# Attention scores of all units as plain float32 products on the two halves of the rows

## The chip, the cores and the metric

The kernel runs on one core of a Trainium2 chip. The metric is the device time of one execution in microseconds (us). A core has a matrix engine (TensorE, PE in the profile; its loads of stationary operands are PEld), VectorE (DVE), ScalarE (ACT), GpSimd (POOL), and SyncE (SP), which here issues nearly all DMAs. A program's instructions stand in a fixed order on each engine, and an instruction that waits holds up all behind it on that engine.

## The reference, cut to what matters

```python
# attention: B=2, H=8, S=576, D=64
scores = scale * np.matmul(q, k.transpose(0, 1, 3, 2))
rel = np.log1p(np.abs(pos[:, None] - pos[None, :]))
x = (rel / np.log1p(np.maximum(pos[:, None], 1.0)))[..., None]
bias = np.maximum(x @ w1 + b1, 0.0) @ w2          # one bias per head, 576 x 576
scores = scores + bias.transpose(2, 0, 1)[None]
attn = softmax(scores)                            # over the last axis
out = attn @ v                                    # then x of 1152 tokens x 512
# two feed-forward layers
x = (silu(x @ w_gate) * (x @ w_val)) @ w_out      # d_ff 1536
x = softplus(x @ w_in) @ w_out2                   # d_ff 2048
```

## The kernel before, in words

The program has three stages on the matrix engine: the bias of all heads, the attention, and the two feed-forward layers, which come last and which the diff does not touch.

**Bias.** 36 steps, one after the other. In each, DVE and ACT make four hidden tiles (`hidden`), PE multiplies them by `W2` on four column strips (`second`, L289), ACT scales the result into a staging tile (`keep`, L302), and SP issues a DMA that spreads the staging tile over rows of `bias[c]`, from SBUF to SBUF. Eight staging tiles go round: four halves of `early[0]` and `early[1]`, and four tiles of the pool `stp`. The last eight steps fill `bias[3]` (`bias_91` in the order lists).

**Attention.** A unit is two heads of one batch (`pr`, `b`); there are eight, in the order of `UNITS`. A unit has two subs (rows 0 to 255 and 256 to 575) and nine chunks of 128 rows by 576 keys; the chunk `mix` holds 64 rows of both heads. `run_slot` is called once for each chunk and does, in this order: the chunk's scores on PE (`scores`), copies of transposes of the slot before (`gather`), bias and minimum on DVE (`biased`, L377), the exponential of the chunk before on ACT and its normalization on POOL (`softmax`, L391 and L399), one or two groups of transposes of a sub that ended three slots ago (`transposes`, L426, four blocks of 128 x 128 as a rule), and, where all of a sub's groups have been copied, its products with the values (`values`, L453). The order on PE, ACT, DVE, POOL and SP is the order in which the code is written (`tc.manual_schedule`). Scores have two PSUM buffers (`psS`): the scores of a slot wait until `biased` of two slots before has read its buffer. Four slots of unit 0 (`EARLY`) are run between bias steps, the others after them.

**Scores of units 1 to 7.** Both halves of the 128 rows hold a copy of the head's 64 dimensions. `prepare_k` and `prepare_q` split keys and queries into float32r high and low parts (`kst`, `qh`, `ql`) on ACT, DVE and POOL (L204, L206, L210), two steps in each slot. A chunk is then four float32r products over all 128 rows (`ql` and `qh` for each half of the 576 keys), the mixed chunk eight (L356).

**Scores of unit 0.** `plain_scores` (L328) takes plain float32 products: each head stands once, in its own half of the rows, and two chunks of different heads are issued together, so that their products use different halves.

**Loads.** `load_k(0)`, `load_v(units[0])` and the first table come at the start. The keys of unit 1 and 256 columns of its queries are loaded between bias steps (`NEXT`), its other query columns and its values at slot 4. A load of both copies of one tensor is two DMAs of 64 rows (L162), 288 KB each; unit 0's are one DMA of 128 rows each (L180).

**Pools.** After the bias steps the pool `ep1` is opened at the right end of SBUF, where `stp` and other tiles of the bias stage stood; the second of the two `mixes` (`m_919`) lies in it, and POOL clears a strip of each (L615).

Of the kernel before, what the change touches and what calls it, by code (L numbers as in the profile page):

```python
# [11 lines left out]
F32 = mybir.dt.float32  # L12
# [7 lines left out]
P = 128  # L20
# [20 lines left out]
NEXT = (20, 28)  # L41

# [3 lines left out]
KHIGH, KLOW = "va", "ppvp"  # L46
QHIGH, QLOW = "vvvavva", "ppppp"
# [53 lines left out]
def tile_kernel(ctx: ExitStack, tc, qT, kT, vS, wb, wg, wv, wo, wi, wo2, table, out):  # L101
# [27 lines left out]
    with ExitStack() as actx:  # L129
# [4 lines left out]
        rawp = opener(right)("qkraw", 1, side="right")  # L134
        kp = pool("kp", 2)
        qp = pool("qp", 1)
# [20 lines left out]
        qraw = pool("qraw", 1)  # L157
        psS = pool("psS", 2, space=PSUM)

        def load(r, src, pr, b, cols=slice(None)):  # L160
            for d in range(2):
                sp.dma_start(  # L162
                    out=r[D * d : D * (d + 1), :, cols],
                    in_=src[b, 2 * pr : 2 * pr + 2, :, cols].rearrange("h d s -> d h s"),
                )

        def load_k(i):

            pr, b = UNITS[i]
            u = dict(i=i, pr=pr, b=b)  # L170
            if i == 1:
                kr = early[3]
            elif i > 2:
                kr = bias[0][:, :2]
            else:
                kr = rawp.tile([P, 2, S], F32, tag="kr", name="kr")
            if i == 0:

                for t, src in ((0, kT), (1, qT)):
                    sp.dma_start(out=kr[:, t], in_=src[b, 2 * pr : 2 * pr + 2].rearrange("h d s -> (h d) s"))  # L180
                u["qr"] = kr[:, 1]
                kr = kr[:, 0]
            else:
                load(kr, kT, pr, b)
            u["kr"] = kr
            return u

        def load_q(u, cols=slice(None)):
            if "qr" not in u:
                u["qr"] = qraw.tile([P, 2, S], F32, tag="qr", name="qr")  # L190
            load(u["qr"], qT, u["pr"], u["b"], cols)
# [10 lines left out]
        def high(h, src, by="a"):  # L202
            if by == "a":
                nc.scalar.copy(h, src)  # L204
            else:
                nc.vector.tensor_copy(h, src)  # L206

        def low(l, h, src, by="p"):
            eng = nc.gpsimd if by == "p" else nc.vector
            eng.tensor_tensor(l, src, h.bitcast(F32), op=ALU.subtract)  # L210

        def prepare_k(u):


            kst = u["kst"] = kp.tile([P, 2, S], F32R, tag="kst", name="kst")
            kr = u["kr"]
            for a in range(2):
                high(kst[:, a], kr[:, a], KHIGH[a])
                yield
                for hf in range(2):  # L220
                    rows, cols = slice(D - D * hf, P - D * hf), slice(HALF * hf, HALF * (hf + 1))
                    low(kst[rows, a, cols], kst[rows, a, cols], kr[rows, a, cols], KLOW[2 * a + hf])
                yield

        def job(sub):
            chunks = [(0, 0), (1, 0), ("mix",), (0, 1), (1, 1)] if sub else [(0, 0), (1, 0), (0, 1), (1, 1)]
            return dict(sub=sub, chunks=chunks, sm=smp.tile([P, 4, 5], F32, name="sm"), es=[], last=[], at={})

        def prepare_q(u, sub):


            qr = u["qr"]
            if u["i"] == 0:
                u[sub] = dict(u, **job(sub))
                return
            width = 704 if sub else 512
            qh = qp.tile([P, width], F32R, tag=f"qh{sub}", name="qh")
            ql = qp.tile([P, width], F32R, tag=f"ql{sub}", name="ql")
            if sub == 0:
                parts = [(0, 0, 0, 256), (1, 256, 0, 256)]  # L240
            else:
                parts = [(0, 0, 256, 320), (1, 384, 256, 320)]
                nc.gpsimd.memset(qh[:, 320:384].bitcast(F32), 0.0)
                nc.gpsimd.memset(ql[:, 320:384].bitcast(F32), 0.0)
            u[sub] = dict(u, qh=qh, ql=ql, **job(sub))
            for j, (a, o, s0, w) in enumerate(parts):
                high(qh[:, o : o + w], qr[:, a, s0 : s0 + w], QHIGH[2 * sub + j])
                yield
                low(ql[:, o : o + w], qh[:, o : o + w], qr[:, a, s0 : s0 + w], QLOW[2 * sub + j])
                yield  # L250
# [5 lines left out]
        stp = pool("stp", 4)  # L256
        early = [xp.tile([P, 2, S], F32, tag=f"a{i}", name=f"early{i}") for i in range(4, 8)]
        spare_st = [t[:, i] for t in early[:2] for i in range(2)]
# [39 lines left out]
        def keep(s, pb):  # L298
            c, t = divmod(s, 8)
            i = order.index(s) % 8  # L300
            st = stp.tile([P, S], F32, name="st") if i % 2 else spare_st[i // 2]
# [9 lines left out]
        def plain_scores(u, *ns):  # L311


            sub, made = u["sub"], []
            for n in ns:
                ch = u["chunks"][n]
                if ch[0] == "mix":
                    heads, bt = [(0, 512, D), (1, 256, D)], bias[4][:, u["pr"]]
                else:
                    a, c = ch  # L320
                    heads, bt = [(a, 256 * sub + D * (sub and a) + P * c, P)], bias[2 * sub + c][:, 2 * u["pr"] + a]
                made.append((psS.tile([P, 2, 512], F32, tag="S", name="ps"), bt, heads))
            for step in range(2):
                for ps, _, heads in made:
                    for a, o, m in heads:
                        rows = slice(D * a, D * (a + 1))
                        hf = (step + a) % 2
                        nc.tensor.matmul(  # L328
                            ps[rows if m == D else slice(None), hf, :HALF],
                            u["qr"][rows, o : o + m],  # L330
                            u["kr"][rows, HALF * hf : HALF * (hf + 1)],
                            start=True,
                            stop=True,
                        )
            return [(ps, bt) for ps, bt, _ in made]

        def scores(u, n):

            sub, pr = u["sub"], u["pr"]
            ch = u["chunks"][n]  # L340
            ps = psS.tile([P, 2, 512], F32, tag="S", name="ps")
            if ch[0] == "mix":
                heads = [(0, 256), (1, 320)]
                bt = bias[4][:, pr]
            else:
                a, c = ch
                heads = [(a, (448 if sub else 256) * a + P * c)]
                bt = bias[2 * sub + c][:, 2 * pr + a]

            if u["i"] == 0:  # L350
                return plain_scores(u, n)[0]
            kst = u["kst"]
            parts = [(t, a, o) for t in ("ql", "qh") for a, o in heads]
            for hf in range(2):
                for i, (t, a, o) in enumerate(parts):
                    nc.tensor.matmul(  # L356
                        ps[:, hf, :HALF],
                        u[t][:, o : o + P],
                        kst[:, a, HALF * hf : HALF * (hf + 1)],
                        start=i == 0,  # L360
                        stop=i == len(parts) - 1,
                    )
            return ps, bt
# [151 lines left out]
        prep = prepare_q(units[0], 0)  # L515
        before = None
        ahead = []
        slot = 0

        def run_slot():  # L520
            nonlocal turned, done, prep, before, slot
            if slot < len(chunks):
                i, sub, n = chunks[slot]
                if n == 0:
                    for _ in prep:
                        pass
                    if sub == 0:
                        if 0 < i < 2 * NP - 1:
                            units.append(load_k(i + 1))
                        if i == NP:  # L530
                            flat = lambda ap: ap.rearrange("p a s -> p (a s)")
                            pairs[2:] = [flat(bias[c][:, 2 * a : 2 * a + 2]) for a in range(2) for c in (2, 3)]
                            mixes[1] = flat(bias[4][:, :2])[:, : 5 * P]
                            nc.gpsimd.memset(mixes[1][:, S:], 0.0)
                        prep = prepare_q(units[i], 1)
                    elif i + 1 < 2 * NP:
                        load_q(units[i + 1], slice(256 if i == 0 else 0, S))
                        load_v(units[i + 1])
                        prep = itertools.chain(prepare_k(units[i + 1]), prepare_q(units[i + 1], 0))
# [21 lines left out]
            for _ in range(2):  # L561
                next(prep, None)
# [578 lines left out]
```

## Time and profile before

| | |
|---|---|
| time of three runs | 601.05, 601.07, 601.9 us; median 601.07 |
| the profiled execution | 601.18 us, of which the span of the trace is 599.4 us |
| busy share of the span | PE 97%, PEld 86%, DVE 76%, ACT 62%, POOL 17% |
| bias stage, attention, feed-forward layers | to about 59 us, to about 200 us, to the end |

Matmuls are pipelined and overlap, so that a busy PE says little; what counts is from the start of one block of products to the start of the next.

### The profile page before, as it was taken

The page shows a single profiled execution, that of the slowest core. Times are in us where ns is not written, and L with a number is a line of the kernel's source. Part 1 is how long each engine was busy: PE and PEld are TensorE (multiplying, and loading weights), DVE is VectorE, ACT ScalarE, POOL GpSimd, SP SyncE. Part 2 cuts the span into 40 slices and gives each one's busy share as a digit, 9 for nine tenths or more (in the row PEclk, how much of TensorE's full clock was granted, in tenths as well). Part 3 has the DMA queues.
Part 4 walks back from the last instruction along what each step waited for, and adds up shares of the span by engine and source line. Part 5 has one row for each costly group of instructions (what it writes and reads, how often), then busy time and mean ns, then how long its engine had stood idle before and what let it go on. Part 6 is the DMA issues. An engine that isn't in the chain of part 4 may idle for free.

```text
span 599.4 us, 11363 instructions
## 1 busy us (share of the span) xinstructions
PE 580.0 (97%) x4274; PEld 515.1 (86%) x4274; DVE 454.9 (76%) x977; ACT 374.6 (62%) x713; POOL 104.6 (17%) x156
## 2 busy tenths in 40 slices
PE   8998399999999999999999999999999999999997
PEld 5444188888887999999999999999989989988986
DVE  6998278878888899888679834679998976983432
ACT  6999187888888877665467525248835734732520
POOL 0001387878995000000000000000000000000000
PEclk9999699999999999999999999999999999999999
DMA  5999734444334243323325222222434340410012
GB/s 191 205 204 204 154 80 111 109 109 109 81 85 152 72 141 98 112 73 108 105 71 176 91 86 70 72 71 72 140 109 136 107 136 7 139 36 1 1 51 107
DMA packets 47414, 62.71 MB, mean 105 GB/s; under 512 B 4480, under 2 KB 35712, under 8 KB 47360
## 3 DMA queue, kind: packets, MB, share of 16 engines
q1 hardware_dynamic: 47216, 61.98, 37.0%
q8 instruction: 33, 0.54, 0.4%
q14 instruction: 21, 0.17, 0.1%
q10 hardware_dynamic: 144, 0.02, 0.0%
HBM read 49.01 MB, written 2.36 MB: 86 GB/s over the span
## 4 chain that ended last, share of the span: by engine, by line
PE 86%; DVE 4%; DMA 3%; POOL 3%; ACT 2%; issue 1%; POOLq 0%; ACTq 0%; SPq 0%
PE pw L748 37%; PE pw L1056 16%; PE pw L699 12%; PE pb L289 6%; PE po L453 5%; PE ps L356 5%; DMA bias<-st 3%; PE pt L426 3%; POOL e L399 1%; PE warm L590 1%; POOL ql L210 1%; DVE bias L377 1%; DVE e L377 1%; ACT at L433 1%; DVE at L433 0%
## 5 line engine op out<-in xcount | busy, mean ns | idle before, releaser
L1056 PE MATMUL pw<-oh,g2h 128*128 128x512 f32 x144 | 56.2, 390 | 0.0
L1056 PE MATMUL pw<-oh,g2l 128*128 128x512 f32 x144 | 56.2, 390 | 0.0
L1056 PE MATMUL pw<-ol,g2h 128*128 128x512 f32 x144 | 56.1, 390 | 0.0
L377 DVE CUSTOM_DVE_ANT_0 e<-ps,bias 128x576 f32<-128x576 f32 x44 | 33.0, 750 | 20.6 <-PE ps L328 12.9
L289 PE MATMUL pb<-r,wb_sb 128*32 128x288 f32 x576 | 47.4, 412 | 0.8 <-ACT st L302 0.7
L699 PE MATMUL pw<-gl,sh 128*128 128x384 f32 x144 | 48.2, 335 | 0.0
L699 PE MATMUL pw<-gh,sl 128*128 128x384 f32 x144 | 48.2, 334 | 0.0
L699 PE MATMUL pw<-gh,sh 128*128 128x384 f32 x144 | 48.2, 334 | 0.0
L281 DVE TENSOR_SCALAR r<-G 128x576 f32<-128x576 f32 x108 | 47.3, 526 | 0.0
L673 DVE SCALAR_TENSOR_TENSOR x<-raw,x 128x512 int32<-128x512 int32 x68 | 46.3, 688 | 0.9
L433 ACT COPY at<-pt 128x512 f32<-128x512 f32 (+2 forms) x69 | 36.3, 548 | 15.4 <-PE pt L426 15.0
L399 POOL TENSOR_SCALAR e<-e,sm 128x576 f32<-128x576 f32 x44 | 33.9, 780 | 64.3 <-DVE sm L396 58.1
L356 PE MATMUL ps<-kst,ql 128*128 128x288 f32 x140 | 43.2, 337 | 1.1 <-DVE sm L377 0.4
L289 PEld LDWEIGHTS pb<-r,wb_sb 128*32 128x32 f32 x576 | 22.5, 109 | 25.0 <-DVE r L281 9.1
L426 PE MATMUL pt<-ident,e 128*128 128x128 f32 x188 | 31.7, 277 | 10.4 <-POOL e L399 10.4
L453 PE MATMUL po<-at,v 128*64 128x256 f32 (+3 forms) x384 | 36.9, 332 | 1.1 <-DVE at L433 0.8
L356 PE MATMUL ps<-kst,qh 128*128 128x288 f32 x140 | 37.4, 295 | 0.0
L1094 DVE TENSOR_TENSOR acc<-pw,acc 128x512 f32<-128x512 f32 x27 | 17.5, 685 | 25.1 <-PE pw L1056 25.1
L391 ACT ACTIVATE e<-e,sm 128x576 f32<-128x576 f32 x44 | 34.4, 781 | 3.4 <-DVE sm L377 2.5
L670 DVE TENSOR_SCALAR x<-x 128x512 int32<-128x512 int32 x68 | 28.8, 428 | 10.1 <-ACT x L669 5.9
L426 PEld LDWEIGHTS pt<-ident,e 128*128 128x128 f32 x188 | 24.0, 143 | 12.5 <-POOL e L399 10.9
L356 PEld LDWEIGHTS ps<-kst,ql 128*128 128x128 f32 x140 | 25.4, 188 | 9.9 <-DVE sm L377 5.0
(276 smaller groups left out, 1674.5 us busy)
## 6 DMA issues: line engine op xcount, KB each, us to landing
raw<-in_wo_dram SPq DMA_DIRECT2D x28, 512.0 KB, 3.6
raw<-in_wi_dram SPq DMA_DIRECT2D x16, 512.0 KB, 3.8
raw<-in_wv_dram SPq DMA_DIRECT2D x12, 512.0 KB, 4.2
raw<-in_wg_dram SPq DMA_DIRECT2D x12, 512.0 KB, 3.6
bias<-early SPq DMA_DIRECT2D x16, 288.0 KB, 7.7
bias<-st SPq DMA_DIRECT2D x16, 288.0 KB, 8.4
qr<-in_qT_dram SPq DMA_DIRECT2D x12, 288.0 KB, 4.1
v<-in_vS_dram SPq DMA_DIRECT2D x8, 384.0 KB, 3.4
```

The lines of the kernel that those rows point to most:

```text
L281: nc.vector.tensor_scalar(r, G[:, w0 : w0 + S], PB[:, n : n + 1], 0.0, op0=ALU.add, op1=ALU.max)
L289: nc.tensor.matmul(pb[32 * ct : 32 * ct + 32, hf, :HALF], W2, rs[ct][:, HALF * hf : HALF * (hf + 1)], start=True, stop=True,)
L356: nc.tensor.matmul(ps[:, hf, :HALF], u[t][:, o : o + P], kst[:, a, HALF * hf : HALF * (hf + 1)], start=i == 0, stop=i == len(parts) - 1,)
L377: nc.vector.tensor_tensor_reduce(out=e[:, :S].rearrange("p (a n) -> p a n", a=2), in0=ps[:, :, :HALF], in1=bt.rearrange("p (a n) -> p a n" ...
L399: nc.gpsimd.tensor_scalar(e, e, sm[:, 3, i : i + 1], 1.0, op0=ALU.mult, op1=ALU.mult)
L426: nc.tensor.transpose(pt[:, P * w : P * (w + 1)], e, ident)
L433: marks[eng, u["i"], u["sub"]] = copy(at[:, :w], pt[:, :w]).ins
L453: nc.tensor.matmul(u["po"][D * a : D * (a + 1), o : o + n], v[:, D * t : D * (t + 1)], at[:, i : i + n], start=piece == 0 and o == 0, stop ...
L673: nc.vector.scalar_tensor_tensor(yi, lw, 29, yi, op0=ALU.logical_shift_right, op1=ALU.bitwise_or)
L699: nc.tensor.matmul(ps[:, :n], w[:, k], x, start=first and k == 0 and i == 0, stop=last and k == NK - 1 and i == 2)
L748: nc.tensor.matmul(ps[:, hf, :HALF], a[:, o + k], b[:, HALF * hf : HALF * (hf + 1)], start=start and k == 0 and i == 0, stop=k == 1 and i ...
L1056: nc.tensor.matmul(ps, g, w.rearrange("p k f -> p (k f)"), start=f == 0 and i == 0, stop=f == 3 and i == 2)
```

## The change

All units' scores become plain float32 products. Keys and queries of every unit, unit 0's too, are loaded twice, a copy in each half of the rows. A chunk is now two products, one in each half of the rows, for the two halves of the keys; the mixed chunk is four, each on a quarter of the array. All high and low parts go, with the instructions that make them. Unit 1's keys and queries are loaded at the start, ahead of the first bias DMA; a later unit's keys, queries and values at the first chunk of the second sub of the unit before it. The staging tiles are eight halves of the four `early` tiles, and both `mixes` lie in `tmpp`.

```diff
+        kqp = pool("kqp", 2)
...
+        def load_kq(i):
+            pr, b = UNITS[i]
+            u = dict(i=i, pr=pr, b=b)
+            for name, src in (("kr", kT), ("qr", qT)):
+                u[name] = kqp.tile([P, 2, S], F32, tag=name, name=name)
+                load(u[name], src, pr, b)
             return u
...
-        stp = pool("stp", 4)
+        staging = itertools.cycle([t[:, i] for t in early for i in range(2)])
...
-            kst = u["kst"]
-            parts = [(t, a, o) for t in ("ql", "qh") for a, o in heads]
-            for hf in range(2):
-                for i, (t, a, o) in enumerate(parts):
-                    nc.tensor.matmul(
-                        ps[:, hf, :HALF],
-                        u[t][:, o : o + P],
-                        kst[:, a, HALF * hf : HALF * (hf + 1)],
-                        start=i == 0,
-                        stop=i == len(parts) - 1,
-                    )
+                parts, bt = [(0, 0, 512), (1, 1, 256), (0, 1, 512), (1, 0, 256)], bias[4][:, pr]
...
+                parts = [(a, hf, o) for hf in range(2)]
+            for a, hf, o in parts:
+                rows = slice(D * hf, D * (hf + 1))
+                to, m = (slice(D * a, D * (a + 1)), D) if ch[0] == "mix" else (slice(None), P)
+                nc.tensor.matmul(
+                    ps[to, hf, :HALF],
+                    u["qr"][rows, a, o : o + m],
+                    u["kr"][rows, a, HALF * hf : HALF * (hf + 1)],
+                    start=True,
+                    stop=True,
+                )
...
-        units, late = [load_k(0)], []
+        units, late = [load_kq(0)], []
         load_v(units[0])
+        units.append(load_kq(1))
...
+                    if i and sub and i + 1 < 2 * NP:
+                        units.append(load_kq(i + 1))
                         load_v(units[i + 1])
...
-            for i, mp in enumerate((tmpp, ep1)):
-                mixes.append(mp.tile([P, 5 * P], F32, name=f"m{i}"))
+            for i in range(2):
+                mixes.append(tmpp.tile([P, 5 * P], F32, name=f"m{i}"))
```

On PE, in unit 1, after the products with the values of unit 0's first sub (`e` and `m` are exponentials, `pt` their transposes, `ps` scores), before:

```order
L453 MATMUL po<-at,vt_99 64x256 x2
L356 MATMUL ps<-kst,ql 128x288
L356 MATMUL ps<-kst,qh 128x288
L356 MATMUL ps<-kst,ql 128x288
L356 MATMUL ps<-kst,qh 128x288
L426 MATMUL pt<-ident,e_909 128x128
L426 MATMUL pt<-ident,e_910 128x128
L426 MATMUL pt<-ident,m_917 128x128
L426 MATMUL pt<-ident,e_909 128x128
```

and of the change, the same place and the next slot:

```order
L350 MATMUL po<-at,vt_93 64x256 x2
L253 MATMUL ps<-kr,qr 128x288 x2
L323 MATMUL pt<-ident,e_881 128x128
L323 MATMUL pt<-ident,e_882 128x128
L323 MATMUL pt<-ident,m_889 128x128
L323 MATMUL pt<-ident,e_881 128x128
L253 MATMUL ps<-kr,qr 128x288 x2
```

The blocks stand in the same order; where four products over the whole array stood there are two over half of its rows, still between transposes over the whole array.

On POOL, at the end of the bias stage, where unit 0's chunks are normalized (TENSOR_SCALAR) and the mixed tiles cleared (MEMSET), with what each waits for (DMAHW is a landing of a DMA), before:

```order
L399 TENSOR_SCALAR e_112<-e_112,sm 128x576 [waits Activation_49]
L615 MEMSET m_917 128x64 [waits DMAHW1_49,Activation_49]
L615 MEMSET m_919 128x64 [waits DMAHW6_49,DMAHW7_49,DMAHW3_49,DMAHW1_49]
L399 TENSOR_SCALAR e_112<-e_112,sm 128x576 [waits DVE_49,Activation_49]
L210 TENSOR_TENSOR kst<-early_131,kst 64x288 [waits DMAHW2_49,DVE_49,Pool_49]
```

and of the change:

```order
L296 TENSOR_SCALAR e_106<-e_106,sm 128x576 [waits Activation_49]
L493 MEMSET m_889 128x64 [waits DMAHW1_49,Activation_49]
L493 MEMSET m_891 128x64 [waits PE_49]
L296 TENSOR_SCALAR e_106<-e_106,sm 128x576 [waits DVE_49,Activation_49]
L296 TENSOR_SCALAR e_881<-e_881,sm 128x576 [waits DVE_49,Activation_49]
```

The second clearing no longer waits for DMAs, and the subtractions for unit 1's keys behind it are gone.

On SP, from the start to the first bias DMA, before:

```order
L264 DMA G<-in_table_dram 128x1064
L180 DMA kr<-in_kT_dram 128x576
L180 DMA kr<-in_qT_dram 128x576
L197 DMA v<-in_vS_dram 128x4x192
L199 DMA vt_99<-in_vS_dram 64x2x64
L200 DMA vt_99<-in_vS_dram 64x64
L309 DMA bias_92<-early_128 16x4x576 x2
```

and of the change:

```order
L191 DMA G<-in_table_dram 128x1064
L155 DMA kr<-in_kT_dram 64x2x576 x2
L155 DMA qr<-in_qT_dram 64x2x576 x2
L171 DMA v<-in_vS_dram 128x4x192
L173 DMA vt_93<-in_vS_dram 64x2x64
L174 DMA vt_93<-in_vS_dram 64x64
L155 DMA kr<-in_kT_dram 64x2x576 x2
L155 DMA qr<-in_qT_dram 64x2x576 x2
L235 DMA bias_86<-early_116 16x4x576 x4
```

Eight loads of 64 rows stand where two of 128 rows stood, and four loads of unit 1 that stood among the bias DMAs (L162) are gone from there.

## Rows read from the trace of the kernel before

**Rows 1.** The page's chain that ended last, shares of the span by engine.

```profile
PE 86%; DVE 4%; DMA 3%; POOL 3%; ACT 2%; issue 1%; POOLq 0%; ACTq 0%; SPq 0%
```

**Rows 2.** Busy time in stretches: PE, PEld, DVE, ACT, POOL, then granted clock, DMA share, GB/s.

```profile
2.00:9.00 7.00, 7.00 (x52) 5.79 (x53) 3.87 (x9) 3.00 (x5) 0.00 (x0) 1.00 0.79 280
8.00:18.00 10.00, 9.96 (x120) 4.75 (x114) 10.00 (x24) 8.88 (x14) 0.00 (x0) 1.00 0.50 138
20.00:57.00 37.00, 36.27 (x444) 17.38 (x434) 36.82 (x89) 35.80 (x58) 0.85 (x1) 1.00 1.05 205
72.00:76.00 4.00, 3.87 (x21) 2.60 (x20) 1.98 (x5) 2.21 (x5) 3.96 (x6) 0.67 0.15 44
92.00:108.00 16.00, 15.58 (x136) 13.04 (x135) 13.36 (x42) 12.63 (x32) 12.56 (x18) 1.00 0.39 101
```

**Rows 3.** The chain that ended last, 57 to 76 us: start, length, what.

```profile
57.29 9.80 DMA bias<-st
67.09 3.11 issue
...
70.35 0.73 POOL e L399
...
75.81 0.80 PE ps L356 x4
```

**Rows 4.** Timeline, 60 to 75 us: who stood idle, and until what, in brackets.

```profile
70.20 0.15 POOL L615 MEMSET m<- 128x64 f32 x1 [11.59 <-issue]
...
71.14 0.48 PE L426 MATMUL pt<-ident,e 128*128 128x128 f32 x1 [10.35 <-POOL e L399]
...
73.87 0.76 DVE L377 CUSTOM_DVE_ANT_0 e<-ps,bias 128x576 f32<-128x576 f32 x1 [11.50 <-PE ps L328]
```

**Rows 5.** DMA queues, 74 to 79 us: packets, MB, share of 16 engines' time.

```profile
q1 hardware_dynamic: 288, 0.59, 44.4%
```

**Rows 6.** The chain that ended last, 77 to 143 us.

```profile
77.36 2.31 PE po L453 x20
...
107.03 0.71 POOL ql L210
...
110.90 2.31 PE po L453 x20
113.21 0.73 PE ps L356 x4
113.94 0.44 PE pt L426 x4
114.37 0.53 PE ps L356 x4
...
116.75 1.05 PE ps L356 x8
...
126.59 2.31 PE po L453 x20
...
143.15 2.31 PE po L453 x20
```

**Rows 7.** Timeline of PE alone in narrow windows at unit 0's plain products.

```profile
38.41 0.41 PE L289 MATMUL pb<-r,wb_sb 128*32 128x288 f32 x2
38.75 0.51 PE L328 MATMUL ps<-kr 64*128 64x288 f32 x2
...
39.10 0.41 PE L328 MATMUL ps<-kr 64*128 64x288 f32 x2
...
59.66 0.41 PE L328 MATMUL ps<-kr 64*64 64x288 f32 x2
...
59.90 0.41 PE L328 MATMUL ps<-kr 64*64 64x288 f32 x2
60.24 0.33 PE L426 MATMUL pt<-ident,e 128*128 128x128 f32 x1
...
60.41 0.38 PE L426 MATMUL pt<-ident,e 128*128 128x128 f32 x2
```

More of the change, by code (lines that the diff above doesn't have):

```diff
@@ L156, in tile_kernel, with load @@
         new_pairs("ep0", 2)
-        qraw = pool("qraw", 1)
         psS = pool("psS", 2, space=PSUM)
-        def load(r, src, pr, b, cols=slice(None)):
+        def load(r, src, pr, b):
             for d in range(2):
                 sp.dma_start(
-                    out=r[D * d : D * (d + 1), :, cols],
-                    in_=src[b, 2 * pr : 2 * pr + 2, :, cols].rearrange("h d s -> d h s"),
+                    out=r[D * d : D * (d + 1)], in_=src[b, 2 * pr : 2 * pr + 2].rearrange("h d s -> d h s")
                 )
-        def load_k(i):
+        def load_kq(i):
             pr, b = UNITS[i]
             u = dict(i=i, pr=pr, b=b)
[L171 to L185, printed above, removed]
-            return u
[L188 to L191, printed above, removed]
+            for name, src in (("kr", kT), ("qr", qT)):
+                u[name] = kqp.tile([P, 2, S], F32, tag=name, name=name)
+                load(u[name], src, pr, b)
+            return u
         def load_v(u):
@@ L225, in job @@
-        def job(sub):
-            chunks = [(0, 0), (1, 0), ("mix",), (0, 1), (1, 1)] if sub else [(0, 0), (1, 0), (0, 1), (1, 1)]
[L227 to L250, printed above, removed]
@@ L252, in tile_kernel, with job @@
+        def job(u, sub):
+            chunks = [(0, 0), (1, 0), ("mix",), (0, 1), (1, 1)] if sub else [(0, 0), (1, 0), (0, 1), (1, 1)]
+            u[sub] = dict(u, sub=sub, chunks=chunks, sm=smp.tile([P, 4, 5], F32, name="sm"), es=[], last=[], at={})
         sctx = actx.enter_context(ExitStack())
@@ L299, in keep @@
             c, t = divmod(s, 8)
-            i = order.index(s) % 8
-            st = stp.tile([P, S], F32, name="st") if i % 2 else spare_st[i // 2]
+            st = next(staging)
             nc.scalar.activation(
@@ L309, in keep @@
                     sp.dma_start(out=bias[c][D * a + t : D * a + t + 61 : 4], in_=st[a::2])
[L311 to L327, printed above, removed]
-                        nc.tensor.matmul(
[L329 to L333, printed above, removed]
-                        )
-            return [(ps, bt) for ps, bt, _ in made]
         def scores(u, n):
@@ L342, in scores @@
             if ch[0] == "mix":
-                heads = [(0, 256), (1, 320)]
-                bt = bias[4][:, pr]
+                parts, bt = [(0, 0, 512), (1, 1, 256), (0, 1, 512), (1, 0, 256)], bias[4][:, pr]
             else:
                 a, c = ch
[L347 to L351, printed above, removed]
-            kst = u["kst"]
-            parts = [(t, a, o) for t in ("ql", "qh") for a, o in heads]
-            for hf in range(2):
-                for i, (t, a, o) in enumerate(parts):
-                    nc.tensor.matmul(
-                        ps[:, hf, :HALF],
-                        u[t][:, o : o + P],
-                        kst[:, a, HALF * hf : HALF * (hf + 1)],
-                        start=i == 0,
-                        stop=i == len(parts) - 1,
-                    )
+                o, bt = 256 * sub + D * (sub and a) + P * c, bias[2 * sub + c][:, 2 * pr + a]
+                parts = [(a, hf, o) for hf in range(2)]
[9 more added lines that the diff above has]
+                )
             return ps, bt
@@ L524, in run_slot @@
                 if n == 0:
[L525 to L537, printed above, removed]
+                    if slot == 4:
+                        load_v(units[1])
+                    if i and sub and i + 1 < 2 * NP:
+                        units.append(load_kq(i + 1))
                         load_v(units[i + 1])
-                        prep = itertools.chain(prepare_k(units[i + 1]), prepare_q(units[i + 1], 0))
+                    if i == NP and sub == 0:
+                        flat = lambda ap: ap.rearrange("p a s -> p (a s)")
+                        pairs[2:] = [flat(bias[c][:, 2 * a : 2 * a + 2]) for a in range(2) for c in (2, 3)]
+                    job(units[i], sub)
                 u = units[i][sub]
-                if ahead:
-                    got = ahead.pop()
-                elif i == 0 and u["chunks"][n][0] == 0:
-                    got, then = plain_scores(u, n, n + 1)
-                    ahead.append(then)
-                else:
-                    got = scores(u, n)
+                got = scores(u, n)
             for w in done:
```

36 lines of the change are left out of this document (2 added, 34 removed).

## The prediction

> **What bounds the kernel now.** I read the chain that ended last first: PE has 86% of it [rows 1], so the question in every stretch is when PE may start its next block. The chain then shows one place where PE does not decide, the change from the bias stage to the attention [rows 3]. From 57 to 67 us it lies on a bias DMA, and the engines start again at 70.2 us. The timeline says who stood there [rows 4]: POOL idle for 11.59 us ahead of clearing the second mixed tile, PE for 10.35 us ahead of a transpose that needs POOL's normalization, DVE for 11.50 us. POOL's wait is marked "issue"; the order list says what it is, landings of DMAs that read the staging tiles. So the last bias row lands at about 70.2 us. The stretches say why so late: from 20 to 57 us the DMA engines are full (share 1.05, 205 GB/s), while from 8 to 18 us they are half idle [rows 2]. After the landing the chain needs another 5.6 us, nearly all POOL (normalizations, low parts of unit 1's keys and queries), until PE starts unit 1's first scores at 75.81 us [rows 3].
>
> From there PE goes from block to block. A slot's scores take 0.53 us to the next block, 0.73 us behind products with the values, the mixed chunk 1.05 us, four transposes 0.44 us [rows 6]. One unit to the next is 16.45 us on average (products with the values of the first sub start at 77.36 and, four units on, at 143.15), and 15.69 us at best (110.90 to 126.59). The 0.76 us between the two are waits; the chain goes to POOL's `ql` at such a place, at 107.03 us [rows 6]. In a stretch of 16 us the other engines are busy 12.6 to 13.4 us [rows 2], so none of them is the bound.
>
> **The change, part by part.** The sum starts from 601.18 us, the profiled execution's own time, 0.1 us above the median.
>
> *The end of the bias DMAs.* Removed from the full stretch: unit 1's keys (576 KB) and 256 query columns (256 KB), 0.85 MB at 205 GB/s, 4.2 us. Added at the start: eight loads of 64 rows in place of two of 128. Two such loads (0.59 MB) take 44.4% of 5 us, 2.2 us of all DMA engines [rows 5]; the same bytes in loads of 128 rows take 1.7 us, from 0.79 of 7 us for 280 GB/s [rows 2]. So 4 x 2.2 - 1.7 = 7.1 us are added, of which 5.0 us fit into the idle half of 8 to 18 us; 2.1 us push the bias DMAs. Net 2.1 us earlier: the last bias row lands at 68.1 us. Bounds: with loads of 64 rows as cheap as those of 128 (1.7 us for two), nothing is pushed and it lands at 66.0; at the 205 GB/s of the bias copies (2.9 us for two) 4.9 us are pushed and it lands at 70.9. I take 2.2 because it is the same form of load. The longer list of loads on SP also stands ahead of the first bias DMA, but the bias steps have eight staging tiles and lose nothing there.
>
> *From the landing to unit 1.* In the changed order POOL's second clearing waits for PE alone, unit 1 needs no low parts, and its keys and queries have long landed. Slots 4 to 6, the scores of slots 7 and 8 and the first transposes run before the landing. What is left behind it is one `biased` (0.76 us, [rows 4]), which frees the score buffer: unit 1's first scores start at 68.9 instead of 75.81 us, 6.9 us earlier. Something is late next: PE has been idle, and its clock will be low. Before, PE started again at 71.14 and the clock was at its lower level until about 74.6 (0.67 granted on average from 72 to 76 us, [rows 2]); PE waited for POOL then, so little was lost. Now the same 3.5 us fall on unit 1's scores and values and cost up to half of them, 1.7 us; I take 1.6 (bounds 0, where the idle time is too short for it, and 3.4). Sum of the hand-over: -5.3 us.
>
> *The scores on PE.* Unit 0's plain products show the price. Two products in different halves of the rows start within 0.01 us of each other (x2 in one row), and pair follows pair by 0.24 us [rows 7]. A float32 product is two passes, so a chunk is 0.48 us of streaming; the four float32r products it replaces take 0.53. But the array is divided differently from the transposes around it, and there the rows show a toll. Entering costs 0.34 instead of 0.24 (38.41 to 38.75), the second pair 0.35 instead of 0.24 (38.75 to 39.10), leaving 0.34 (59.90 to 60.24), and the first transpose 0.17 instead of 0.11 [rows 7]; together 0.35. A block between transposes so takes 0.83 us against 0.53, +0.30; behind products with the values it already paid 0.20, so 0.83 against 0.73, +0.10. The mixed chunk's four products lie on four quarters; if all go at once, as four strips do in the bias stage, 0.83 against 1.05, -0.22. By the order list every block is followed by transposes. Seven units: 42 x 0.30 + 14 x 0.10 - 7 x 0.22 = +12.5 us. The bounds: no toll, -22 us from this; or 0.20 both ways, as between values and scores, +3 us more.
>
> A rule of the Trainium skill speaks against the change here: TensorEngine Tiling (Array Packing), section Key Properties, says that changing the tiling mode, and not just the tile, drains the engine. The trace agrees, with 0.10 us on the way in and as much on the way out. The page has no price.
>
> *The work taken from DVE, ACT and POOL.* Six subtractions, five to six conversions and two clearings in each unit go. It hides under PE but for the waits it causes: 0.76 us in a unit. PE's blocks get longer and the other engines' queues shorter, so I give all of it back, 7 x 0.76 = -5.3 us (bounds 0 and -5.3).
>
> *Nothing else.* The feed-forward layers run as before, 395 us behind the attention, with PE full.
>
> Sum: 601.18 - 5.3 + 12.5 - 5.3 = 603.1 us.
>
> **The rivals.**
>
> *The early loads gain nothing.* At the 205 GB/s of the bias copies [rows 2] two loads of 64 rows take 2.9 us, the last row lands at 70.9, after the 70.2 of before, and the time is 2.8 us longer, **605.9**. For it: 2.2 us is already more than the 1.7 of full loads. Against it: that row is of the same form. A rule of the Trainium skill would bring it about, SBUF — State Buffer, section Door 1: 64 partitions reach eight of the sixteen ports, some 218 GB/s; by it, as an estimate, one load is 1.35 us, two 2.7. The trace has 2.2 us of engine time for two.
>
> *The quarters go two at a time.* Then the mixed chunk is 0.48 us longer, **606.5**. For it: unit 0's mixed chunk went in pairs; against it: it used two quarters only.
>
> *The waits in the units stay*: up to **608.4**. For it: some end on DVE's `biased` and on copies, not on the parts.
>
> *Faster, by the early loads.* If they cost what loads of 128 rows cost, the last row lands at 66.0, unit 1 starts at 66.8, and PE's idle time is then hardly longer than the 3.6 us after which its clock fell before, so that the clock may stay: -2.1 - 1.6, **599.4**. It decides from a landing before 66.5 us on. For it: the DMA engines are idle just then; against it: the row of 2.2.
>
> *No toll.* If PE hid the change of the array's division between transposes and scores, a block would take 0.48: 22 us less, and with the engines' other waits back **581 to 587**. That is also the Trainium skill's promise on the same page, Theoretical Speedup: up to 2x for contractions of 64. The rows contradict it, on the way in and on the way out [rows 7].
>
> **How the numbers follow.** My forecast has 0.50, its own range 600 to 606.5, from the bounds of clock (1.6 us each way) and waits. Early loads without gain 0.12, pairs 0.13, waits that stay 0.07, faster by the early loads 0.14, no toll 0.04. The predicted time is 603.1. A measurement can tell 0.2% (1.2 us) here: slower is above 602.3, faster below 599.9. Slower: 0.30 of the forecast and 0.31 of the next three, 0.61. Faster: 0.03 of the forecast, 0.11 of the fourth, 0.04 of the last, 0.18. The rest, 0.21, is the same. The range 598 to 609 leaves out the last case and the tails.
>
> **What would show it.** In the changed profile: the DVE `biased` of slot 7 at about 68 us, not 73.87; first scores of unit 1 about a microsecond later; a lower clock just there; a block of scores 0.83 us long between transposes; POOL busy under 9 of 16 us; units 17.2 us apart. I am wrong if units stay at 16.5 us or less (no toll), if the landing is not before 70 (loads), or if the units are over 17.8 us apart (quarters, waits).

## The result, and the profile after

The changed kernel takes 606.19 us (median of four runs, 604.42 to 607.21) where the kernel before took 601.26 (601.05 to 601.9): 1.0077 times as long, 95% interval 1.0051 to 1.0103, slower. I had said 603.1, and 598 to 609. The profiled execution took 607.21 us with a span of 605.4, 6.0 us above that of before.

The chain that ended last, shares of the span by engine, as in [rows 1]:

```profile
PE 91%; DMA 7%; ACT 1%; DVE 0%; issue 0%; POOL 0%; ACTq 0%; DVEq 0%; SPq 0%; POOLq 0%
```

POOL's 3% and DVE's 4% are gone: from unit 1's first scores (71.01 us) to the first feed-forward product (205.09 us) PE waits once, for 0.7 us. Busy time in stretches, with the columns of [rows 2]:

```profile
8.00:18.00 10.00, 9.96 (x120) 4.80 (x120) 10.00 (x24) 9.36 (x15) 0.00 (x0) 1.00 1.06 242
68.00:72.00 4.00, 0.99 (x4) 0.57 (x4) 1.56 (x5) 1.01 (x3) 0.00 (x0) 0.50 1.10 198
72.00:76.00 4.00, 4.00 (x18) 1.82 (x18) 2.70 (x11) 3.17 (x8) 2.68 (x4) 0.50 0.66 161
76.00:80.00 4.00, 4.00 (x26) 2.17 (x22) 0.77 (x2) 0.69 (x3) 0.28 (x1) 0.77 0.00 0
92.00:108.00 16.00, 16.00 (x135) 10.13 (x134) 10.53 (x33) 11.28 (x29) 6.18 (x9) 1.00 0.37 87
```

Three things are to be seen. The DMA engines, half idle from 8 to 18 us before, are full there now (share 1.06). The granted clock is 0.50, the 1.2 GHz level, from 68 to 76 us, while PE works all of the last four. And from 92 to 108 us PE is busy 16.00 of 16 us, with POOL at 6.18 instead of 12.56. The timeline at the hand-over, in the form of [rows 4]:

```profile
59.77 0.23 POOL L493 MEMSET m<- 128x64 f32 x2
70.19 0.76 DVE L274 CUSTOM_DVE_ANT_0 e<-ps,bias 128x576 f32<-128x576 f32 x1 [7.82 <-DMA vt<-in_vS_dram]
71.01 1.40 PE L253 MATMUL ps<-kr,qr 64*128 64x288 f32 x4 [6.33 <-DVE sm L274]
```

Both clearings run at 59.77 us and hold nobody. But `biased` of slot 7, the first work that needs the last bias row, starts at 70.19 us, the moment at which POOL was let go before (70.20, [rows 4]): `biased` starts no sooner than that. The row names a load of unit 1's values, `vt`, as what DVE waited for, and so does the chain. It can't be that one. Two rows of what SP issues from 50 to 72 us, with the median time from issue to landing:

```profile
bias<-early SPq DMA_DIRECT2D x7, 288.0 KB, 10.4
vt<-in_vS_dram SPq DMA_DIRECT2D x1, 32.0 KB, 10.9
```

`vt`, issued at 61.46 us, has landed only at 72.4. The last bias DMA, issued at 59.28 us, landed at about 69.8, where it was about 70.1 before, and DVE goes through the rest of its waits until 70.19. The chain from there on, to be read beside [rows 3, 6]:

```profile
71.01 1.40 PE ps L253 x4
...
73.02 1.26 PE ps L253 x4
74.28 4.08 PE po L350 x20
...
94.64 2.31 PE po L350 x20
96.95 0.69 PE ps L253 x4
97.63 0.59 PE pt L323 x4
98.22 0.69 PE ps L253 x4
98.91 1.02 PE pt L323 x8
...
101.20 0.65 PE ps L253 x8
...
111.94 2.31 PE po L350 x20
...
146.55 2.31 PE po L350 x20
...
205.09 1.78 PE pw L626 x12
```

and two rows of the same view of before that [rows 6] does not have:

```profile
94.18 2.38 PE po L453 x20
...
199.97 1.79 PE pw L748 x12
```

So the 6.0 us come about as follows. Unit 1's first scores start 4.80 us earlier (75.81 to 71.01). Its first values start only 3.08 us earlier (77.36 to 74.28), because the two blocks of scores and the two transposes between them took 3.27 us at the lower clock, where they took 1.55 before. The values then take 4.08 us instead of 2.31, and PE's tolls in this unit come on top, so that the next values (94.18 before, 94.64 after) are already 0.46 us late. From there to the first feed-forward product it is 110.45 us instead of 105.79, 4.66 more: one unit follows another by 17.30 us (94.64 to 111.94, and 17.30 on average to 146.55) instead of 16.45. The last 0.9 us lie behind the last sum on DVE (`acc`), at the end of the program; this execution was the longest of the four.

### The profile page after: what moved, and what is told of

The parts are those of the page before. It is cut to its first block, busy times and chain, and to the rows that moved or that the text cites. A ratio compares the mean times of both kernels' runs of the same rounds, so it can differ in the third digit from the quotient of the medians.

```text
span 605.4 us, 11232 instructions
## 1 busy us (share of the span) xinstructions
PE 587.2 (97%) x4274; PEld 490.0 (81%) x4274; DVE 439.2 (73%) x942; ACT 370.5 (61%) x699; POOL 62.4 (10%) x92
## 4 chain that ended last, share of the span: by engine, by line
PE 91%; DMA 7%; ACT 1%; DVE 0%; issue 0%; POOL 0%; ACTq 0%; DVEq 0%; SPq 0%; POOLq 0%
PE pw L626 37%; PE pw L934 16%; PE pw L577 12%; PE ps L253 7%; PE po L350 7%; PE pt L323 7%; DMA bias<-early 5%; PE pb L216 3%; DMA vt<-in_vS_dram 1%; ACT early L228 1%; PE warm L472 1%; ACT r L206 0%; PE ps L323 0%; ACT e L288 0%; DVE e L274 0%
## 5 line engine op out<-in xcount | busy, mean ns | idle before, releaser
L253 PE MATMUL ps<-kr,qr 64*128 64x288 f32 (+1 forms) x320 | 55.0, 456 | 6.7 <-DVE sm L274 6.7
L216 PE MATMUL pb<-r,wb_sb 128*32 128x288 f32 x576 | 44.8, 412 | 4.6 <-ACT early L228 3.8
L216 PEld LDWEIGHTS pb<-r,wb_sb 128*32 128x32 f32 x576 | 18.5, 109 | 29.8 <-ACT early L228 14.8
L253 PEld LDWEIGHTS ps<-kr,qr 64*128 64x128 f32 (+1 forms) x320 | 21.5, 177 | 23.7 <-issue 11.7
L350 PE MATMUL po<-at,v 128*64 128x256 f32 (+3 forms) x384 | 38.4, 342 | 0.7 <-DVE at L330 0.7
L323 PEld LDWEIGHTS pt<-ident,e 128*128 128x128 f32 x188 | 20.6, 141 | 18.8 <-issue 9.7
L350 PEld LDWEIGHTS po<-at,v 128*64 128x64 f32 x384 | 27.2, 140 | 9.0 <-issue 3.7
L323 PE MATMUL pt<-ident,e 128*128 128x128 f32 x188 | 33.8, 288 | 0.1
```

Source lines behind the costliest of these rows:

```text
L216: nc.tensor.matmul(pb[32 * ct : 32 * ct + 32, hf, :HALF], W2, rs[ct][:, HALF * hf : HALF * (hf + 1)], start=True, stop=True,)
L253: nc.tensor.matmul(ps[to, hf, :HALF], u["qr"][rows, a, o : o + m], u["kr"][rows, a, HALF * hf : HALF * (hf + 1)], start=True, stop=True,)
L323: nc.tensor.transpose(pt[:, P * w : P * (w + 1)], e, ident)
L350: nc.tensor.matmul(u["po"][D * a : D * (a + 1), o : o + n], v[:, D * t : D * (t + 1)], at[:, i : i + n], start=piece == 0 and o == 0, stop ...
```

## The experiments

All times are medians of four to twelve runs beside runs of the kernel before, whose median moved between 600.5 and 601.7 us. Differences to the changed kernel are therefore taken between ratios to the kernel before, where it has 1.0077.

### The toll on PE

**Transposes in halves of the rows.** If PE pays for changing the division of the array, transposes with the scores' division should make the toll go.

```diff
-                nc.tensor.transpose(pt[:, P * w : P * (w + 1)], e, ident)
+                for h in range(2):
+                    r = slice(D * h, D * (h + 1))
+                    nc.tensor.transpose(pt[:, h, D * w : D * (w + 1)], e[r], ident[r, r])
```

> The changed kernel, but each 128x128 transpose is made of two over 64 rows, into two PSUM banks, so that transposes divide the array as the scores do; one gather still copies a piece (now from two banks), and there are two places for pieces in PSUM instead of three. Theory A (the toll of 0.35 us for a block comes from changing the array's division): scores 0.48 to 0.53 us instead of 0.69, four transposes 0.22 (if the halves go at once) to 0.44 instead of 0.59, units 17.3 - 9 x 0.35 = 14.2 us apart or a little less, until ACT or the places in PSUM bind; 580 to 586 us. Rival B (the toll belongs to plain float32 products, wherever they stand): scores stay at 0.69, units no closer than 16.5, 600 us or more. If halves of a transpose don't overlap, four take about 0.9 and the unit gains nothing: 606.

Measured: 615.84 us, ratio 1.0254 (1.0231 to 1.0278). The chain of this kernel, and what PE waited for from 84 to 195 us (total, times, longest):

```profile
109.61 0.69 PE ps L253 x4
110.29 0.51 PE ptw L326 x16
...
115.02 0.54 PE ps L253 x4
```
```profile
PE ptw L326 <- ACT at L333: 11.0, 16, 1.7
PE ptw L326 <- DVE at L333: 8.7, 11, 1.7
```

The prices are those of theory A. Eight transposes, as sixteen halves, take 0.51 us instead of 1.02, and scores between them 0.54 instead of 0.69; only behind values, whose products divide the array by columns, is it still 0.69. The time is not: PE waits 19.7 of 111 us for gathers, with only two places for pieces, and the granted clock falls in between (0.79 from 92 to 108 us). The toll is shown, and with it that it is no gain by itself to take it away.

**Four places instead of two.** The values take one of the two score tiles, and the bank that this frees makes two more places.

```diff
-                u["po"] = psO.tile([P, 512], F32, name="po")
+                u["po"] = psS.tile([P, 2, 512], F32, tag="S", name="ps")[:, 0]
...
+            ptw = [psT.tile([P, 2, 512], F32, name="ptw") for _ in range(2)]
```

> The changed kernel with transposes in halves of the rows as in the first experiment, but four places for transposed pieces in PSUM instead of two; for that the products with the values have no bank of their own and take one of the two score tiles, and the two subtractions that read them stand together. Theory A (the toll is the change of division, and the first experiment lost its gain to waits for places): scores 0.54, four transposes 0.25, no waits for gathers above 0.5 us; the score tile held by the values costs about 1.2 us twice in a unit, so units 15 to 15.5 us apart: 588 to 595 us. Rival B (gathers on ACT and DVE, or the score tile held by the values, are as long as PE's blocks): units at 17 or more, 604 us or more.

Measured: 609.82 us, ratio 1.0163 (1.0145 to 1.0181); rival B. Stretch and waits of PE:

```profile
108.00:200.00 92.00, 75.10 (x946) 52.73 (x946) 61.42 (x198) 69.67 (x166) 41.41 (x55) 1.00 0.38 98
```
```profile
PE ps L253 <- DVE sm L274: 7.7, 14, 0.7
PE ptw L326 <- DVE at L333: 6.0, 6, 1.3
PE ptw L326 <- ACT at L333: 3.5, 6, 1.0
```

PE has 75 us of work in 92, ACT 70 and DVE 61; none is full, and the unit still takes over 17 us. My reading of the chain, which no run tests by itself, is that with short blocks on PE the unit is set by the rounds from scores over `biased`, exponential, normalization and gather back to PE, two score tiles deep. How much of it another order of DVE's and ACT's work would give back was not tried.

**Two by two.** The same work with fewer changes of division.

```diff
-TWICE = (4, 8)
+PER_SLOT = (2, 0, 2, 0, 2, 0, 2, 1, 2)
...
-            for _ in range(2 if slot % 9 in TWICE or over else 1):
+            for _ in range(2 if over else PER_SLOT[slot % 9]):
```

> The changed kernel with the same scores and transposes in another order: eleven pieces of transposes in a unit stand two at a time in five slots and one in a sixth, and three slots have none, so that three score blocks in a unit follow another without transposes between. Theory A (0.35 us for each time that the array's division changes and changes back): 3 x 0.35 = 1.05 us less in a unit, units 16.3 us apart, 599 us. Rival B (the toll belongs to the blocks, not to the changes between them): units at 17.3, 606 us. If two score blocks in a row wait for DVE's biased, the gain is smaller by that wait: 601 to 604.

Measured: 602.38 us, ratio 1.0024 (1.0012 to 1.0037), 3.2 us less than the changed kernel. Its chain:

```profile
94.32 1.02 PE pt L323 x8
95.34 1.17 PE ps L253 x8
96.51 1.02 PE pt L323 x8
```

Two blocks of scores and eight transposes take 1.17 + 1.02 = 2.19 us, where apart they take 2 x (0.69 + 0.59) = 2.56: 0.37 for each change avoided, against the 0.35 that I had. Units come 16.7 to 16.9 us apart (values at 91.25, 107.97 and 124.91 us) and not 16.3, since PE now waits in some places for `biased` and for DVE's subtractions. The toll belongs to the change, not to the block; the gain was half given back, the third reading that I had put down.

**Whole rows.** What a block takes when its products use all rows; values and mixed chunks still divide the array by columns.

```diff
-                rows = slice(D * hf, D * (hf + 1))
+                rows = slice(0, P)
```

> The changed kernel with every score product over all 128 rows (so each score is counted twice, which changes the output) and the same number of products; only the mixed chunks still divide the array, by columns. It tells what going at once on two halves gives back, and what the change of division takes. Theory A (0.24 us for each float32 pass of 288 columns; the toll belongs to the change of division): a block is four passes one behind the other, 0.96 to 1.0 us, and four transposes behind it take 0.44 again: 1.40 to 1.45 us together against 1.28 now, units 18.3 to 18.8 apart, 613 to 616 us. Rival B (the toll belongs to plain float32 products beside transposes): 0.96 + 0.21 and 0.59, 1.76 us together, units above 21 apart, 632 us or more.

Measured: 619.15 us, ratio 1.0294 (1.0269 to 1.0320). Its chain:

```profile
95.73 0.97 PE ps L253 x4
96.70 0.44 PE pt L323 x4
97.14 2.31 PE po L350 x20
```

A block takes 0.97 us, and the transposes behind it 0.44, as in [rows 6]: 1.41 together, theory A, no toll. I had the total 3 us too low, since blocks behind values still pay 0.2 and the mixed chunks pay theirs. So going at once on two halves gives PE 0.48 us for a block (two of its four passes of 0.24), and the change of division takes about 0.35 of them.

### The hand-over

**Loads of all rows.** Are the loads of 64 rows what keeps the last landing at 70 us?

```diff
-            for d in range(2):
+            for h in range(2):
                 sp.dma_start(
-                    out=r[D * d : D * (d + 1)], in_=src[b, 2 * pr : 2 * pr + 2].rearrange("h d s -> d h s")
+                    out=r[:, h], in_=src[b, 2 * pr : 2 * pr + 2].rearrange("h d s -> (h d) s")
```

> The changed kernel with every load of keys and queries of all 128 rows (both heads, twice) instead of one half of the rows with both heads: as many loads and bytes, but rows 64 to 127 hold the other head's data, so the scores are of wrong rows. Theory A (a load of 64 rows takes 1.23 us where one of 128 takes 0.8, and the eight at the start push the bias DMAs by that): the last load of unit 1 lands at 14 to 15 us instead of 17.73, the last bias row at 66.5 to 67.5 instead of 69.8, unit 1's first scores 2.5 to 3 us earlier, 603 us. Rival B (the bias steps or SP's queue set the last landing): 69 to 70 us as now, 606.

Measured: 600.92 us, ratio 1.0000 (0.9988 to 1.0012), 4.6 us less than the changed kernel. What SP issues, first in the changed kernel, then here:

```profile
8.59 1.83 SPq L155 DMA_DIRECT2D qr<-in_qT_dram  x2
11.12 7.29 SPq L235 DMA_DIRECT2D bias<-early  x8
```
```profile
7.43 1.19 SPq L155 DMA_DIRECT2D qr<-in_qT_dram  x2
9.14 6.27 SPq L235 DMA_DIRECT2D bias<-early  x8
```

By then each issue stands behind a landing some eight DMAs back, so that the time between rows is that of loads: 2.53 us for two of 64 rows, 1.71 for two of 128. `biased` of slot 7 starts at 65.20 us instead of 70.19. With loads of all rows the time is that of the kernel before: the form of the loads is worth as much as the whole loss, and it is won at the hand-over, where `biased` starts 4.99 us earlier.

That bears out the rule by which I had worked out a rival: the Trainium skill, SBUF — State Buffer, section Door 1, says that 64 partitions reach eight of the sixteen ports. By its figure one such load is 1.35 us, an estimate; the trace has 1.26, and 0.86 for as many bytes in all rows. That it is the ports, no run here shows.

**Unit 1's loads back among the bias steps.**

```diff
-        units.append(load_kq(1))
...
+                if i == 24:
+                    units.append(load_kq(1))
```

> The changed kernel, with unit 1's four loads of keys and queries put back among the bias steps (after step 24 of 36) instead of ahead of the first. Theory A (early loads fill DMA time that stood idle from 8 to 18 us): the DMA engines idle there again for 3 to 5 us, the last bias row lands at 73 to 74 instead of 69.8, unit 1's first scores 3 to 4 us later, 609 us. Rival B (the place doesn't matter, since the loads take as much of a full queue in either): landing at 69.8, 606 us.

Measured: 606.98 us, ratio 1.0102 (1.0082 to 1.0122), 1.5 us more than the changed kernel, with intervals that overlap; `biased` of slot 7 at 71.88 us instead of 70.19. From 8 to 18 us:

```profile
8.00:18.00 10.00, 9.96 (x119) 4.79 (x114) 10.00 (x24) 8.96 (x14) 0.00 (x0) 1.00 0.96 219
```

The DMA engines are nearly full there even without unit 1's loads: unit 0's four loads of 64 rows have taken most of the time that I had counted on. The early place gains 1.7 us at `biased`, between the two theories. Little of it is left behind unit 1's first values, which end at 78.80 us instead of 78.37: the clock came back sooner here (0.88 from 76 to 80 us, against 0.77), and they took 2.81 us, not 4.08.

**The same loads early in the kernel before.**

```diff
         load_v(units[0])
+        units.append(load_k(1))
+        load_q(units[1], slice(0, 256))
...
-                if i == NEXT[0]:
-                    units.append(load_k(1))
-                if i == NEXT[1]:
-                    load_q(units[1], slice(0, 256))
```

> The kernel before, with unit 1's loads (keys, and the 256 query columns) ahead of the first bias DMA instead of among the bias steps; nothing else. Theory A (they fill DMA time that stands idle there, 3.7 us of loads): the last bias row lands at 66.5 to 67.5 instead of 70.1, and all behind it is earlier by as much, 598 us. Rival B (as in the changed kernel they push the bias DMAs by what they take): landing at 69.5 to 70, 601 us.

Measured: 596.05 us, ratio 0.9922 (0.9909 to 0.9935). The last link of the bias stage in its chain, and the stretch:

```profile
57.09 7.42 DMA bias<-st
64.78 0.74 POOL e L399
```
```profile
8.00:18.00 10.00, 9.96 (x122) 4.78 (x116) 10.00 (x24) 9.44 (x15) 0.00 (x0) 1.00 1.00 236
```

The last row lands at 64.5 us, 5.6 earlier, more than the 3.7 us of loads that were moved. So the idle half was there, and it takes in about what unit 1's loads need when unit 0 is loaded in two loads of 128 rows. The changed kernel puts twice the bytes for unit 0 and all of unit 1's queries into it, in the dear form, and lands about 5.3 us later than this.

**The clearing alone.** In the kernel before, the second clearing on POOL stands seven slots later.

```diff
-                nc.gpsimd.memset(mixes[-1][:, S:], 0.0)
+                if i == 0:
+                    nc.gpsimd.memset(mixes[-1][:, S:], 0.0)
...
+                if slot == 11:
+                    nc.gpsimd.memset(mixes[1][:, S:], 0.0)
```

> The kernel before, with one edit: the clearing of the second mixed tile, which waits for all staging DMAs, stands on POOL seven slots later (behind unit 1's low parts). It takes the hand-over's part of the change alone. Theory A (the clearing held POOL, and POOL held unit 1): normalizations and low parts run before the last landing at 70.1, unit 1's first scores at about 71 instead of 75.81, less what the lower clock takes, about 3: 599 us. Rival B (ACT's conversions of unit 1's keys stand behind exponentials that wait for the landing too): POOL's low parts stay behind the landing, first scores at 74 to 75, 600 to 601 us.

Measured: 598.89 us, ratio 0.9958 (0.9945 to 0.9971). Its chain:

```profile
71.73 1.30 PE ps L356 x4
...
74.42 3.69 PE po L453 x20
```

Unit 1's first scores start at 71.73 us instead of 75.81: 4.1 of the 4.8 us that the change won at this place come from letting POOL go, and need none of its new products. The lower clock takes its part here too (values 3.69 us).

**A busy wait.** Is it the lower clock that made unit 1 slow?

```diff
+                if slot == 9:
+                    fill = psO.tile([P, 512], F32, name="po")
+                    for _ in range(50):
+                        nc.tensor.transpose(fill[:, :P], ident, ident)
                 run_slot()
```

> The changed kernel, with 50 transposes of the identity (5.5 us) on PE ahead of unit 1's first scores, into a PSUM tile that nothing reads, so that PE isn't idle while it waits for the last bias row. Theory A (the lower clock after the wait costs unit 1 more than I put down): the clock stays at 2.4 GHz from 68 to 78 us, scores there take 0.69 instead of 1.40 and 1.26, the values 2.31 instead of 4.08, the values of unit 1 start at 73.0 instead of 74.3 and end 3.1 us earlier: 603.1 us. Rival B (the lower clock is hidden by other waits): scores are fast but wait for biased and exponentials, 605 to 606.

Measured: 603.52 us, ratio 1.0047 (1.0029 to 1.0065), 1.8 us less by the ratios and 2.7 by the medians; the intervals overlap, so that the rows have to decide. The stretches, and the first values:

```profile
68.00:72.00 4.00, 3.55 (x30) 2.76 (x29) 1.78 (x7) 1.27 (x4) 0.00 (x0) 1.00 1.10 192
72.00:76.00 4.00, 4.00 (x32) 2.24 (x32) 2.80 (x10) 3.12 (x9) 2.96 (x4) 1.00 0.67 157
```
```profile
72.63 2.31 PE po L350 x20
```

The clock stays at its upper level, and the first values end at 74.94 us instead of 78.37, though the row lands as late as before. The lower clock cost about 3 us here.

**Toll and clock together**, the paired order with the busy wait.

> The changed kernel with the paired order of scores and transposes and with the 50 transposes of the identity ahead of unit 1's first scores. If toll and clock are separate costs, the two gains add: 606.2 less 3.8 less 2.7 is 599.7 us, about the kernel before. If part of the gain of the paired order came from a shorter time at the lower clock (its profile shows scores of 1.40 and values of 4.46 us there, so it didn't), the sum is smaller: 601 to 602 us.

Measured: 599.65 us, ratio 0.9990 (0.9980 to 1.0000): the two gains add, as forecast (599.7).

**What is left when only the hand-over is taken over.** The kernel before with early loads and late clearing, then with 20 transposes of the identity ahead of unit 1's first scores as well.

> The kernel before with both gains of the hand-over and without the plain products in the other units: unit 1's loads ahead of the first bias DMA, and the second clearing on POOL seven slots later. Theory A (landing and clearing are two causes, one behind the other): the last bias row lands at 64.5 us as with the loads alone, POOL's normalizations and low parts run ahead of it, unit 1's first scores start at about 66 us instead of 70.9, at a clock that has hardly had time to fall: 4 to 5 us less than the 596.05 of the loads alone, 592 us. Rival B (POOL's low parts wait for keys and queries or for ACT's conversions anyway): first scores at 69 to 70, 594 to 596 us.

> The kernel before with early loads, late clearing, and 20 transposes of the identity (2.2 us) on PE ahead of unit 1's first scores, where PE stood idle for 2.77 us. Theory A (the lower clock from 68 to 72 us, 0.57 granted, costs unit 1 about 2 us there): scores and values at full clock, 590 us. Rival B (the engines behind PE set the pace there): 592 to 593 us as without.

Measured: 592.50 us, ratio 0.9868 (0.9850 to 0.9885), and 591.52 us, ratio 0.9843 (0.9823 to 0.9863). Chain of the first, and the stretch from 68 to 72 us in the first and in the second:

```profile
66.00 0.76 DVE e L377
66.91 0.78 PE ps L356 x4
...
68.89 3.67 PE po L453 x20
```
```profile
68.00:72.00 4.00, 4.00 (x22) 2.44 (x24) 2.75 (x11) 3.25 (x9) 3.71 (x7) 0.57 0.35 86
```
```profile
68.00:72.00 4.00, 4.00 (x34) 3.04 (x34) 2.93 (x12) 3.34 (x10) 3.95 (x8) 1.00 0.24 61
```

The last version is 1.6% faster than the kernel before and 2.3% faster than the changed one. The busy wait gave 1.0 us by the medians and 1.5 by the ratios, of the 2 expected; the intervals overlap. The high and low parts of float32r stay in it.

## Why the prediction came out as it did

The direction and the range were right, the mechanism on PE was right to a few hundredths, and the hand-over was judged 4 us too well.

*The scores on PE: right.* I had 0.83 against 0.53 for a block between transposes, +0.30. The chain puts the toll partly on the transposes: 0.69 + 0.59 = 1.28 us against 0.53 + 0.44 = 0.97 [rows 6], +0.31. Behind values it is 1.28 against 0.73 + 0.44, +0.11 (I had +0.10). The mixed chunk with its three transposes is shorter by about a quarter of a microsecond, as said, so its four quarters go at once, and the rival of two at a time is out. That the cause is the change of division is shown by three runs: it goes with transposes in halves and with whole rows, and shrinks by 0.37 for each change avoided. "No toll" is out with it.

*The waits in the units: right.* PE is busy 16.00 of 16 us. The sum had 1.03 us more for a unit, which from 16.45 is 17.48; the sentence on what would show it said 17.2, a slip of mine. It is 17.30. The unit of 15.69 us, which I took for one without waits, still held some: one of its blocks, at 118.12 us, took 0.70 us instead of 0.53.

*The end of the bias DMAs: the step that failed.* I had the last row at 68.1 us; it lands at about 69.8, where it was 70.1 before. Two sizes were off. Two loads of 64 rows take 2.5 us and not 2.2. And the idle half of 8 to 18 us takes in little of them: I had 5.0 of 7.1 us fit, with 2.1 left to push the bias DMAs, but against the kernel before with early loads (64.5 us) the changed loads push by some 5.3. They eat nearly all that moving unit 1's loads gave, which was more than I had (5.6, not 4.2). Here my first rival, by which the early loads gain nothing, was nearer on the landing (70.9); that its 605.9 us so nearly meets the measured time is luck, since it had the clock at the same 1.6 us. The fourth, by cheap loads, was near on the landing that they would give (66.0; with loads of all rows `biased` starts at 65.2 us), but not on the clock, which it let stay: with PE waiting 3.65 us there, the granted clock was 0.61 from 64 to 68 us and 0.53 from 68 to 72, and the time is 600.9 against the 599.4 I had for it.

*From the landing to unit 1.* `biased` and then scores: 0.8 us, as said. The first scores are 4.80 us earlier instead of 6.9; of the 2.1 us between, 1.7 are the landing, and 0.4 lie between it and the start of `biased`. The step that came late next, the lower clock, was named but mis-sized: 1.6 us put down, 3.3 in the rows (0.71 and 0.57 on two blocks of scores, 0.25 on the transposes between them, 1.77 on the values), near my bound of 3.4. The run with the busy wait agrees: from unit 1's first scores to the end of its first values it takes 4.19 us, the changed kernel 7.36. I had taken 3.5 us at the lower clock from before, where PE started at 71.14 and had its clock back by 74.6. After, it starts at 71.01 and the values that end at 78.37 run almost to their end at the lower one.

Hand-over (2.1) and clock (1.7) together are 3.8 us too well. The units give 0.6 of it back: from unit 1's first scores to the first feed-forward product it is 134.08 us instead of 124.16, which is 9.92 more, and 6.6 without the clock's 3.3, where the sum had 12.5 less 5.3, or 7.2. The rest, 3.2, is the 3.1 us between 603.1 and 606.2.

## What to carry over

Read the rows at a place where the array changes its division before halving work on PE: here two halves at once saved 0.48 us of a block and the way in and out took 0.35, and in place of the float32r form that is a loss. An early load is free only as long as the stretch that it goes into is idle, and its form decides how much of that it takes; compare the landing of the last thing that waits, not the bytes. And take a change apart: the clearing on one engine and the place of four loads were worth 1.3% without the new products, which cost more than they gave.

## What the runs showed of the hardware

In the kernel before with early loads and late clearing PE waited 2.77 us ahead of unit 1's first scores, with shorter waits just ahead of that, and the granted clock fell behind it (0.57 from 68 to 72 us). In the changed kernel, after a wait of 6.33 us, it stayed at 1.2 GHz for some 7 us of full work. In the run with the busy wait PE did nothing but transposes from 64 us to the landing at 70, and the granted clock was 1.00 throughout and after it. The Trainium skill, TensorE: Matmul & The Clock Gate, Part 4, says that the full clock doesn't engage for transposes; here it was up already, and that transposes kept it up is all that this shows.

Transposes of 128x128 in two halves of the rows went twice as fast as whole ones (0.51 us for eight instead of 1.02). And the granted clock fell with no wait for pieces above 1.7 us, when PE was interrupted often, in the kernel with two places for pieces:

```profile
92.00:108.00 16.00, 12.90 (x128) 8.56 (x130) 9.23 (x28) 10.11 (x25) 5.32 (x7) 0.79 0.33 75
```

With as much work in the same stretch (12.87 of 16 us) the kernel with four places kept 1.00; why the one fell and not the other was not settled.
